# Moving the first routing table, the step-2 transposes and the loop's gathers and transposes in a three-part transformer kernel

## The chip, the cores and the metric

The kernel runs on one core of a Trainium2 chip. The metric is device time in microseconds (us), taken over three runs of the kernel; beside it stands one execution that the hardware profiler recorded. TensorE is PE in the rows (PEld is its weight load), VectorE is DVE, ScalarE is ACT, GpSimd is POOL, and SyncE is SP, whose sequencer issues most of the DMAs.

## The reference

Three operations follow one another. The input is `q`, `k`, `v` of 4 batches, 8 heads, 768 positions and 64 dimensions, with 8 memory keys and values per head.

```python
attn = banded_attention(q, k, v, mem_k, mem_v)         # chunks of 32, 16 left, 8 right, plus memory
x = attn.transpose(0, 2, 1, 3).reshape(3072, 512)
h = x @ w_in                                           # 512 x 2048
g = np.where(h >= 1, h, np.where(h <= -1, 0, (h + 1) ** 2 / 4))
x = g @ w_out                                          # 2048 x 512
logits = normed(x) @ normed(expert_emb).T / tau        # 8 experts
e = argmax(logits); gate = softmax(logits)[e]
out = gate * (np.maximum(x @ w1[e], 0) @ w2[e])        # 512 x 1024 x 512 for each token's expert
```

## The kernel before

Tokens are cut into 8 blocks of 384 (`NB`, three tiles of 128 each). For a block, PE runs attention, then the first layer in 16 chunks of 128 features (`l1_mm`, 12 matmuls of 384 columns per chunk, line 444), then the second layer (`l2_mm`, lines 470 to 472). Each chunk of the first layer leaves PSUM by five instructions: ACT at line 450, DVE at 456 and 460, ACT at 463, DVE at 466. Its PSUM tile comes from a ring of three (`mm`) or of two (`PT`) and is free again when DVE has done line 456. After a block the tokens are routed: `g_logit`, `g_first`, `g_pos` find each token's expert and its rank in that expert.

The experts then run in steps of 256 tokens of one expert. Steps 0 and 1 take only tokens of the first 18 tiles (`TA = 18`, blocks 0 to 5), so that they can begin before block 7 is routed. Their tokens are looked up by the first routing table, the tasks `fac` to `fat`: a count on PE, the keys and places on DVE (`fa_key`, `fa_look`, `fa_place`, the last writes tile `fasv`), 18 small matmuls on PE that gather the token numbers (`fai`, function `fa_ids`, line 940), and the table itself on DVE (`fat`, function `fa_table`, 12 instructions, lines 955 to 1009). The second table (`fbc` to `fbt`) does the same for steps 2 and up.

A step `s` needs four things. `gather(s)` (POOL, line 1130) fetches its token rows from DRAM into `xg`. `transposes(s)` or the task `inputs(s)` (SP, line 1142) turns `xg` into `xhl` by two DMA transposes. `load_w` (SP, lines 1111 and 1113) brings eight pieces of an expert's weights of 512 KB each into `stg`; from step 2 on a piece is loaded only where the expert differs from the one before. `split_w` (ACT, line 1117) and `split_lo` (DVE, line 1122) cut each piece into two f16 halves, into the buffers `wi` for even steps and `wo` for odd ones. Then PE runs four chunks of the first product (`m2_l1`, lines 1156, 1157, 1159), each drained by ACT at 1165 and DVE at 1170, and eight parts of the second (`m2_l2`, lines 1185 to 1187), scaled by ACT at 1194 and stored by POOL at 1197.

Each engine runs its instructions in the order in which they were recorded, and SP's queue does so too: a transpose that waits for its gather holds all loads recorded behind it. Up to and with step 2 and the weight splits of step 3 the order comes from a planner (`Plan`): tasks with needs and costs (`COST`) are listed, and a schedule by those costs sets the order on every engine. From step 3 on the order is written out by hand: `at(n, f, ...)` calls `f` when PE's n-th part is recorded, and a step has 12 such parts, starting at `p = first2 + 12 * s`. In step `s` the loop records the split of piece `c` of the next step at part `1 + c`, the reload of its buffer one part later, the gather of the next step and its transposes.

Of the kernel before, what the change touches and what calls it, by code (L numbers as in the profile page):

```python
# [20 lines left out]
B, H, S, D = 4, 8, 768, 64  # L21
# [10 lines left out]
TB = BT // 128  # L32
# [16 lines left out]
    td=1.25, avc=1.3, avp=0.68, av=0.52, xh=0.38, xl=0.47, ca=(0.58, 0.43), cv=0.34, cb=0.6, cs=0.6, cc=0.53, cd=0.6,  # L49
    l1=0.98, r4=0.47, mu=0.47, mn=0.47, hi=0.43, lo=0.47, l2=1.95, l2t=1.3, x2=0.49, sq=0.62, x2l=0.6, xt=1.25, dot=0.65,  # L50
    pad=0.4, emb=0.5, esq=0.6, ert=0.9, ein=1.9, etr=0.4, ehi=0.2, elo=0.2, grt=0.9, gno=1.6, glo=1.2, gfi=1.5, gst=0.8,
    grk=0.1, gpo=1.7, ga=2.6, w=2.3, wh=0.95, wl=1.13, xd=1.25, m1=2.62, mh=0.49, ml=0.6, m2=1.3, mo=0.57, ms=1.0, fbc=0.193,
    fbk=2.2, fbm=1.87, fbl=3.4, fbp=2.1, fbi=0.7, fbt=3.4, fac=0.175, fak=2.6, fal=1.4, fap=0.42, fai=0.5, fat=1.436)
LAT = (0.25, 1.7, 0.1)
WIN = 0.019
# [98 lines left out]
def moe_chain(ctx, tc, qd, kd, vd, win, wout, emb, tau, w1, w2, tmask, kmask, qp, kp, cf32, cf16, out):  # L154
# [506 lines left out]
    def mixture():  # L661
# [4 lines left out]
        def add(k, n, f, where, needs=(), cost=None, ring=None, frees=()):  # L666
            done[k, n] = pl.add((k, n), f, where, COST[cost or k], [x if isinstance(x, dict) else done.get(x) for x in needs], ring, frees)
# [85 lines left out]
        def inputs(s, needs):  # L753

            old = {0: [], 1: [("l1", NB - 1, NFC - 1, 1)], 2: [("m1", 0, 3), ("mo", (0, 1))]}[s]
            for i in range(2):
                add("xd", (s, i), lambda w, i=i: (i == 0 and t_new(s), t_dma(s, i)), "S", [("ga", s), ("xd", (s, i - 1)), *old, *needs])
# [36 lines left out]
        for j in range(NB):  # L794
            i = start[j] + 2 * NFC
            if j == 0:
                for c in range(NFC):
                    conv(c)
            if j == NB - 1:
                n = (("fat", 0),)  # L800
            else:
                n = ()
            for fc in range(NFC if j != 1 else 0):
                first(j, fc, n)
                if j == NB - 1 and fc == 0:
                    for h in range(2):
                        add("ga", h, lambda w, h=h: gather(h), "G", [prev, ("ga", h - 1)])
                    for c in range(8):
                        add("w", c, lambda w, c=c: load_w(0, c), "S", [prev, ("w", c - 1)])
                if j == NB - 1 and fc % 2 == 1:  # L810
                    weights(0, fc // 2, [prev])
                    if fc == NFC - 1:
                        inputs(0, [prev])
            if j + 1 < NB and j != 1:
                for u in range(UB * (j + 1), UB * (j + 2)):
                    attention(u)
            if j == 0:
                for c in range(NFC, 2 * NFC):
                    conv(c)
                for fc in range(NFC):  # L820
                    k = dict(ring="mm", frees=[("x2l", t) for t in range(TB)]) if fc == 0 else {}
                    pe_slot(("l2", 0, fc), i + fc, [("cd", NFC + fc), ("lo", fc), ("hi", fc)], "l2", **k)

                    if fc >= AHEAD:
                        first(1, fc - AHEAD)
                for fc in range(NFC - AHEAD, NFC):
                    first(1, fc)
                for u in range(2 * UB, 3 * UB):
                    attention(u)
                cds = [("cd", c) for c in range(2 * NFC)]  # L830
                add("pad", 0, lambda w: pads(), "G", cds)
                add("emb", 0, lambda w: emb_load(), "S", [("cf", 0)])
                add("esq", 0, lambda w: emb_sq(), "A", [("emb", 0)])
                add("ert", 0, lambda w: emb_root(), "G", [("esq", 0)])
                add("ein", 0, lambda w: emb_inv(), "D", [("ert", 0)])
                add("etr", 0, lambda w: emb_tr(), "P", [("ein", 0)], ring="mm", frees=[("elo", 0)])
                add("ehi", 0, lambda w: emb_hi(), "A", [("etr", 0)])
                add("elo", 0, lambda w: emb_lo(), "D", [("ehi", 0)])
            for t in range(TB):
                n = TB * j + t  # L840
                if j > 0:
                    for fc in range(0, NFC, 2):
                        m = NFC * j + fc
                        k = dict(ring="mm", frees=[("x2l", n)]) if fc == 0 else {}
                        pe_slot(("l2", j, t, fc), i, [("lo", m), ("lo", m + 1)], "l2t", **k)
                        i += 1
                last = ("l2", j, t, NFC - 2) if j else ("l2", 0, NFC - 1)
                add("x2", n, lambda w, n=n: l2_ev(n, p2[n % TB]), "A", [last, ("gst", j - 2), ("x2", n - 1), ("pad", 0)])
                add("sq", n, lambda w, n=n: g_sq(n, p2[n % TB]), "A", [("x2", n), ("sq", n - 1), ("glo", j - 2)])
                add("x2l", n, lambda w, n=n: l2_lo(n, p2[n % TB]), "D", [("x2", n), ("sq", n)])  # L850
                add("xt", n, lambda w, n=n: g_xt(n), "S", [("x2l", n), ("dot", j - 1), ("xt", n - 1)])
            add("grt", j, lambda w, j=j: g_root(j), "G", [("sq", n)])
            add("gno", j, lambda w, j=j: g_norm(j), "D", [("grt", j), ("ein", 0)])
            add("dot", j, lambda w, j=j: g_dot(j), "P", [("xt", n), ("elo", 0), ("gno", j)], ring="mm", frees=[("glo", j)])
            add("glo", j, lambda w, j=j: g_logit(j), "D", [("gno", j), ("dot", j), ("gpo", j - 2), ("gst", j - 2)])
            add("gfi", j, lambda w, j=j: g_first(j), "D", [("glo", j), ("gfi", j - 1)])
            add("gst", j, lambda w, j=j: g_store(j), "D", [("gfi", j)])
            add("grk", j, lambda w, j=j: g_rank(j), "P", [("gfi", j), ("mk", 0)], ring="mm", frees=[("gpo", j)])
            add("gpo", j, lambda w, j=j: g_pos(j), "D", [("grk", j), ("gpo", j - 1)])
            if (j + 1) * TB == TA:  # L860
                add("fac", 0, lambda w: fa_count(), "P", [("gfi", j)], ring="S", frees=[("fak", 0)])
                add("fak", 0, lambda w: fa_key(), "D", [("fac", 0)])
                add("fal", 0, lambda w: fa_look(), "D", [("fak", 0), ("gpo", j)])
                add("fap", 0, lambda w: fa_place(), "D", [("fal", 0)])
                add("fai", 0, lambda w: fa_ids(), "P", [("fap", 0)], ring="S", frees=[("fat", 0)])
                add("fat", 0, lambda w: fa_table(), "D", [("fai", 0)])
        for c in range(8):
            weights(1, c, [("l2", NB - 1, TB - 1, 2 * c)])
        inputs(1, [])
# [10 lines left out]
        second(1)  # L880
        for c in range(8):
            weights(2, c, [("fbt", 0), ("m1", 0, 3) if c < NK else ("m2", 0, 1, c - NK)])
        inputs(2, [])
        second(2)
        for c in range(8):
            weights(3, c, [("m1", 1, 3) if c < NK else ("m2", 1, 1, c - NK)])
# [77 lines left out]
    def fa_count():  # L964
        fa["c"] = T(ps, [128, NE], F32, "S", 2)
        pe.matmul(fa["c"], ones, rs[:, TA, :], start=True, stop=True)

    def fa_key():
        f = small(NE, "faf")
        rounded(f, fa["c"], -127.5, 1.0 / ST)  # L970
        cum = running(cf[:, C_TR:C_TR + 64].rearrange("p (e f) -> p e f", e=NE), f, "fac")
        b = small(NE, "fab")
        dve.tensor_tensor(b, cum, f, ALU.subtract)
        na = small(NE, "fana")
        dve.tensor_scalar(out=na, in0=b, scalar1=-1.0, scalar2=float(NSTA), op0=ALU.mult, op1=ALU.add)
        dve.tensor_tensor(na, na, f, ALU.min)
        dve.tensor_scalar(out=na, in0=na, scalar1=0.0, scalar2=2.0, op0=ALU.max, op1=ALU.mult)
        dve.tensor_scalar(out=f, in0=f, scalar1=2.0, scalar2=None, op0=ALU.mult)
        dve.tensor_scalar(out=b, in0=b, scalar1=2.0, scalar2=None, op0=ALU.mult)
        fa.update(na2=na, cum=cum, b=b, f=f)  # L980

    def fa_look():
        kb, ft = looked(TA, (fa["b"], "fakb"), (fa["f"], "faft"))
        dve.tensor_tensor(kb, kb, q7a[:, 0:TA], ALU.add)
        dve.tensor_tensor(ft, q7a[:, 0:TA], ft, ALU.is_ge)
        dve.scalar_tensor_tensor(out=kb, in0=ft, scalar=100.0, in1=kb, op0=ALU.mult, op1=ALU.add)
        fa.update(kb=kb)

    def fa_place():
        fa["sv"] = placed(fa["kb"], TA, 2 * NSTA, "fa")  # L990

    def fa_ids():
        fa["ip"] = ids_mm(fa["sv"], TA, 2 * NSTA)
# [221 lines left out]

    for s in range(NSTA, NST0 - 1):
        p = first2 + SL * s
        for c in range(8 if s > NSTA else 0):
            split_at(p + 1 + c, s + 1, c)
        at(p + 1, gather, s + 1)  # L1220
        at(p + 5, transposes, s + 1)

    p2 = {}

# [134 lines left out]
```

## Time and profile before

| | |
|---|---|
| time, median of three runs (lowest to highest) | 931.65 us (930.45 to 932.08) |
| the profiled execution: its own time | 933.45 us |
| its span, from the first to the last instruction | 931.7 us |
| PE busy | 867.6 us (93%) |
| DVE busy | 693.2 us (74%) |
| ACT busy | 557.2 us (60%) |
| POOL busy | 73.7 us (8%) |
| mean granted TensorE clock | 0.993 |

Busy shares are means over the whole span. PE's is high from the first eighth of the span to its end, while the others change from stage to stage, so the places that matter are those at which PE stood idle or ran at its lower clock.

### The profile page before, as it was taken

The page shows a single profiled execution, that of the slowest core. Times are in us where ns is not written, and L with a number is a line of the kernel's source. Part 1 is how long each engine was busy: PE and PEld are TensorE (multiplying, and loading weights), DVE is VectorE, ACT ScalarE, POOL GpSimd, SP SyncE. Part 2 cuts the span into 40 slices and gives each one's busy share as a digit, 9 for nine tenths or more (in the row PEclk, how much of TensorE's full clock was granted, in tenths as well). Part 3 has the DMA queues.
Part 4 walks back from the last instruction along what each step waited for, and adds up shares of the span by engine and source line. Part 5 has one row for each costly group of instructions (what it writes and reads, how often), then busy time and mean ns, then how long its engine had stood idle before and what let it go on. Part 6 is the DMA issues. An engine that isn't in the chain of part 4 may idle for free. (4 is left out here: it accounts for less than half of the span.)

```text
span 931.7 us, 17019 instructions
## 1 busy us (share of the span) xinstructions
PE 867.6 (93%) x6072; PEld 522.0 (56%) x6072; DVE 693.2 (74%) x1600; ACT 557.2 (60%) x1398; POOL 73.7 (8%) x70
## 2 busy tenths in 40 slices
PE   2899999999998999999999989999998999999985
PEld 2766555545544644555554544555665667666653
DVE  6999999999999998988872780795745655566550
ACT  4768757979887858749653341465145555555541
POOL 0000100000000000000000100200122222222210
PEclk9999999999999999999999999999999999999998
DMA  9986513767277437424112001583232232223540
GB/s 255 237 178 202 183 62 99 170 190 175 64 159 208 107 99 183 99 89 81 32 44 49 12 35 30 187 238 91 69 82 68 63 87 70 69 69 81 156 140 25
DMA packets 118700, 105.64 MB, mean 113 GB/s; under 512 B 92286, under 2 KB 92548, under 8 KB 118608
## 3 DMA queue, kind: packets, MB, share of 16 engines
q1 hardware_dynamic: 114608, 91.80, 38.3%
q0 software_dynamic: 4000, 12.69, 4.3%
q8 instruction: 49, 0.80, 0.4%
q14 instruction: 43, 0.35, 0.1%
HBM read 112.09 MB, written 12.94 MB: 134 GB/s over the span
## 5 line engine op out<-in xcount | busy, mean ns | idle before, releaser
L444 PEld LDWEIGHTS <-wi 128*128 128x128 f16 x1536 | 148.2, 99 | 98.9 <-issue 5.7
L444 PE MATMUL mm<-xhl,wi 128*128 128x384 f16 x912 | 160.7, 328 | 1.2 <-ACT xhl L383 0.6
L470 PE MATMUL mm<-wo,g 128*128 128x512 f16 x384 | 146.1, 381 | 0.0
L471 PE MATMUL mm<-wo,g 128*128 128x512 f16 x384 | 145.6, 379 | 0.0
L472 PE MATMUL mm<-wo,g 128*128 128x512 f16 x384 | 145.5, 379 | 0.0
L444 PE MATMUL PT<-xhl,wi 128*128 128x384 f16 x624 | 111.3, 331 | 0.0
L1170 DVE SCALAR_TENSOR_TENSOR g<-PT,g 128x512 f16<-128x512 f32 (+1 forms) x52 | 34.8, 670 | 94.2 <-ACT g L1165 94.2
L463 ACT ACTIVATE g<-r 128x384 f16<-128x384 f32 x128 | 66.9, 523 | 60.6 <-DVE r L460 60.3
L1165 ACT ACTIVATE g<-PT 128x512 f16<-128x512 f32 (+1 forms) x52 | 30.2, 580 | 72.8 <-PE PT L1159 72.8
L1122 DVE SCALAR_TENSOR_TENSOR wi<-stg,wi 128x1024 f16<-128x1024 f32 x56 | 66.0, 1219 | 7.9 <-ACT wi L1117 7.9
L466 DVE TENSOR_TENSOR g<-r,g 128x384 f16<-128x384 f32 x128 | 70.3, 549 | 1.0 <-ACT g L463 0.6
L460 DVE SCALAR_TENSOR_TENSOR r<-r,t 128x384 f32<-128x384 f32 x128 | 70.5, 551 | 0.3
L345 ACT ACTIVATE ab<-e,rc 96x128 f16<-96x128 f32 x184 | 58.7, 398 | 16.7 <-issue 11.2
L309 ACT ACTIVATE e<-S,mx 96x128 f32<-96x128 f32 x184 | 64.2, 363 | 5.6 <-DVE mx L293 5.4
L472 PEld LDWEIGHTS <-g 128*128 128x128 f16 x384 | 37.6, 98 | 45.5 <-issue 0.3
L1122 DVE SCALAR_TENSOR_TENSOR wo<-stg,wo 128x1024 f16<-128x1024 f32 x48 | 56.4, 1220 | 8.4 <-ACT wo L1117 8.0
L470 PEld LDWEIGHTS <-g 128*128 128x128 f16 x384 | 37.5, 98 | 38.6 <-issue 0.2
L471 PEld LDWEIGHTS <-g 128*128 128x128 f16 x384 | 37.6, 98 | 36.0
L479 DVE SCALAR_TENSOR_TENSOR x2a<-mm,x2a 128x512 f16<-128x512 f32 x24 | 16.4, 684 | 55.1 <-ACT junk L487 55.0
L1117 ACT ACTIVATE wi<-stg 128x1024 f16<-128x1024 f32 x56 | 56.9, 1047 | 0.6 <-DMA stg<-w 0.6
L1194 ACT ACTIVATE o<-mm,xg 128x512 f32<-128x512 f32 x25 | 17.2, 687 | 66.2 <-issue 41.9
L450 ACT ACTIVATE r<-mm,two 128x384 f32<-128x384 f32 x76 | 43.8, 577 | 19.5 <-PE mm L444 16.1
(262 smaller groups left out, 1791.5 us busy)
## 6 DMA issues: line engine op xcount, KB each, us to landing
stg<-w SPq DMA_DIRECT2D x104, 512.0 KB
kraw<-kd SPq DMA_DIRECT2D x23, 512.0 KB
qraw<-qd SPq DMA_DIRECT2D x23, 384.0 KB
vraw<-vd SPq DMA_DIRECT2D x30, 256.0 KB
x2d<-x2a SPq DMA_DIRECT2D x8, 780.0 KB
x2a<-win SPq DMA_DIRECT2D x8, 512.0 KB
x2a<-wout SPq DMA_DIRECT2D x7, 512.0 KB
kraw<-kp SPq DMA_DIRECT2D x7, 256.0 KB
```

The source lines that it names most:

```text
L309: act.activation(e[:QU, i, :], w["s"][:QU, i, :], AF.Exp, bias=nb[:QU, i:i + 1], scale=0.125 if plain(a // 2) else 1.0, accum_out=sm[:QU, ...
L345: act.activation(w["ab"][:QU, 0, i, :], w["e"][:QU, i, :], AF.Copy, scale=w["rc"][:QU, i:i + 1])
L444: pe.matmul(l1p[fc], w[fc][:, k, :], x[:, k, :], start=(part == 0 and n == 0), stop=(part == 1 and n == 5))
L450: act.activation(g32[fc], l1p[fc], AF.Relu, bias=two[:, 0:1], scale=2.0 ** -13)
L460: dve.scalar_tensor_tensor(out=r4, in0=r4, scalar=4.0, in1=t4s.pop(fc), op0=ALU.min, op1=ALU.mult)
L463: act.activation(gh[fc], g32[fc], AF.Copy)
L466: dve.tensor_tensor(gl[fc], g32.pop(fc), gh[fc], ALU.subtract)
L470: pe.matmul(p, gh[fc][:, ts], woh[fc], start=(fc == 0), stop=False)
L471: pe.matmul(p, gh[fc][:, ts], wol[fc], start=False, stop=False)
L472: pe.matmul(p, gl[fc][:, ts], woh[fc], start=False, stop=(fc == NFC - 1))
L1117: act.activation(hi, stg[c], AF.Copy, scale=64.0 if c < NK else 512.0)
L1122: dve.scalar_tensor_tensor(out=lo, in0=stg[c], scalar=sc, in1=hi, op0=ALU.mult, op1=ALU.subtract)
```

## The change

Four edits. The tasks of the first routing table are listed behind block 6's first layer and no longer at the end of block 5, and `fai` has a new need: the second half of chunk 13 of that layer (`("l1", j, NFC - 3, 1)`). The planner's cost of a gather (`ga`) goes from 2.6 to 5.6. Step 2's transposes have a new need: the fourth weight load of that step (task `w` 19). In the loop, the next step's gather is recorded at part 0 and not 1, its transposes at part 3 and not 5.

```diff
-    grk=0.1, gpo=1.7, ga=2.6, ...
+    grk=0.1, gpo=1.7, ga=5.6, ...
@@ after the first layer of block j
+            if j * TB == TA:
+                add("fac", 0, lambda w: fa_count(), "P", [("gfi", j - 1)], ring="S", frees=[("fak", 0)])
+                add("fak", 0, lambda w: fa_key(), "D", [("fac", 0)])
+                add("fal", 0, lambda w: fa_look(), "D", [("fak", 0), ("gpo", j - 1)])
+                add("fap", 0, lambda w: fa_place(), "D", [("fal", 0)])
+                add("fai", 0, lambda w: fa_ids(), "P", [("fap", 0), ("l1", j, NFC - 3, 1)], ring="S", frees=[("fat", 0)])
+                add("fat", 0, lambda w: fa_table(), "D", [("fai", 0)])
@@ at the end of block j
-            if (j + 1) * TB == TA:
-                add("fac", 0, ...) to add("fat", 0, ...): the same six, with fai's needs [("fap", 0)]
@@ step 2
-        inputs(2, [])
+        inputs(2, [("w", 19)])
@@ the loop over steps s
+        at(p, gather, s + 1)
         for c in range(8 if s > NSTA else 0):
             split_at(p + 1 + c, s + 1, c)
-        at(p + 1, gather, s + 1)
-        at(p + 5, transposes, s + 1)
+        at(p + 3, transposes, s + 1)
```

**PE in block 6's first layer.** `PT` and `wi04` are the PSUM tile and the weights of a chunk, `S` and `fasv` those of the table's 18 small matmuls (one pair of 18 shown). Before:

```order
L444 LDWEIGHTS wi14_90
L444 MATMUL PT_7014<-xhl_5538,wi14_90 128x384
L940 LDWEIGHTS rhot_74
L940 MATMUL S_7037<-fasv_7031,rhot_74 128x4
...
L444 LDWEIGHTS wi04_82
L444 MATMUL PT_7064<-xhl_5538,wi04_82 128x384
```

Now:

```order
L444 LDWEIGHTS wi07_85
L444 MATMUL PT_7145<-xhl_5538,wi07_85 128x384
L940 LDWEIGHTS rhot_74
L940 MATMUL S_7157<-fasv_7031,rhot_74 128x4
...
L444 LDWEIGHTS wi17_93
L444 MATMUL PT_7145<-xhl_5538,wi17_93 128x384
```

They stood behind chunk 8 and now stand inside chunk 14, nearly six chunks later. The count on PE and the DVE instructions up to `fasv` keep their places; the 12 of `fa_table` move from behind chunk 8's line 460 to behind chunk 13's, between the evacuations of chunks 13 and 14.

**ACT in steps 2 and 3.** L1117 splits a piece (`wi_81` to `wi_85` are pieces 3 to 7 of step 2, `wo_94` those of step 3, from `stg_7402` on), L1165 drains a chunk of step 2's first product, L1194 is a scaling of step 2's second product:

```order
 L1117 ACTIVATE wi_81<-stg_7405 128x1024
 L1117 ACTIVATE wi_82<-stg_7406 128x1024
-L1165 ACTIVATE g<-PT 128x2x256
-L1117 ACTIVATE wi_83<-stg_7407 128x1024
+L1117 ACTIVATE wi_83<-stg_7407 128x1024
+L1117 ACTIVATE wi_84<-stg_7408 128x1024
 L1165 ACTIVATE g<-PT 128x2x256 x2
-L1117 ACTIVATE wi_84<-stg_7408 128x1024
-L1165 ACTIVATE g<-PT 128x2x256
-L1117 ACTIVATE wi_85<-stg_7409 128x1024
+L1117 ACTIVATE wi_85<-stg_7409 128x1024
+L1165 ACTIVATE g<-PT 128x2x256
```

Pieces 5 and 6 of step 2 now go ahead of the first drain. Behind these rows piece 0 of step 3 stands ahead of the last drain of step 2 and piece 1 behind it; piece 2 moves ahead of the second L1194, so that five splits of step 3 (pieces 3 to 7) stand behind it and not six. DVE's splits move in the same way.

**SP from step 4 on.** `xhl` is the next step's input, `stg` the reloaded pieces of the step after it. Before:

```order
L1113 DMA stg2_7404<-w1 128x1024
L1113 ISA
L1113 DMA stg3_7405<-w1 128x1024
L1142 DMA_TRANSPOSE xhl_9030<-xg0_7410 128x8x128
L1142 DMA_TRANSPOSE xhl_9030<-xg1_7411 128x8x128
```

Now:

```order
L1113 DMA stg1_7403<-w1 128x1024
L1142 DMA_TRANSPOSE xhl_9009<-xg0_7410 128x8x128
L1142 DMA_TRANSPOSE xhl_9009<-xg1_7411 128x8x128
L1113 ISA
L1113 DMA stg2_7404<-w1 128x1024
```

The transposes stand behind two reloads and not four. On POOL the order of gathers and stores is the same as before. Step 3's two transposes stood ahead of all eight loads of step 3 and now stand behind its first; step 2's stood behind its first and second load and now stand behind its fifth and sixth.

## Rows read from the trace of the kernel before

**Rows 1.** The page: busy time (share) and instructions by engine.

```profile
PE 867.6 (93%) x6072; PEld 522.0 (56%) x6072; DVE 693.2 (74%) x1600; ACT 557.2 (60%) x1398; POOL 73.7 (8%) x70
```

**Rows 2.** Waits of PE: engine, tile, line, releaser: total us, times, longest.

```profile
PE S L940 <- DVE fasv L934: 4.1, 1, 4.1
...
PE PT L1156 <- DMA xhl<-xg: 3.2, 1, 3.2
PE PT L1156 <- ACT wo L1117: 1.9, 2, 1.3
```

**Rows 3.** Timeline, PE, block 6's first layer: start, us, instruction, count, [idle before <-releaser].

```profile
532.62 2.11 PE L444 MATMUL PT<-xhl,wi 128*128 128x384 f16 x12
...
538.86 0.61 PE L940 MATMUL S<-fasv,rhot 128*128 128x4 f16 x18 [4.13 <-DVE fasv L934]
539.33 3.77 PE L444 MATMUL PT<-xhl,wi 128*128 128x384 f16 x12
...
552.70 2.11 PE L444 MATMUL mm<-xhl,wi 128*128 128x384 f16 x12
```

**Rows 4.** Stretches: us; PE, PEld, DVE, ACT, POOL busy; granted clock; DMA share, GB/s.

```profile
539.60:543.00 3.40, 3.40 (x13) 1.58 (x11) 3.26 (x13) 0.52 (x1) 0.00 (x0) 0.50 0.62 234
144.50:147.00 2.50, 0.41 (x5) 0.31 (x5) 2.44 (x4) 2.16 (x11) 0.00 (x0) 1.00 0.00 0
147.10:150.40 3.30, 3.30 (x17) 2.09 (x16) 3.29 (x11) 1.33 (x3) 0.00 (x0) 0.50 0.78 246
...
714.00:726.00 12.00, 8.45 (x67) 6.13 (x66) 8.78 (x9) 9.33 (x11) 4.48 (x3) 1.00 0.22 68
```

**Rows 5.** Timeline, DVE, block 6's first layer.

```profile
540.82 0.55 DVE L456 SCALAR_TENSOR_TENSOR t<-PT,r 128x384 f32<-128x384 f32 x1
...
542.22 0.17 DVE L955 TENSOR_TENSOR faet<-fac,cf 128x16 f32<-128x16 f32 x1
...
544.21 0.55 DVE L456 SCALAR_TENSOR_TENSOR t<-PT,r 128x384 f32<-128x384 f32 x1
...
545.80 0.56 DVE L456 SCALAR_TENSOR_TENSOR t<-mm,r 128x384 f32<-128x384 f32 x1
```

**Rows 6.** Timelines, ACT, DVE and PE, steps 2 and 3.

```profile
697.29 0.60 ACT L1165 ACTIVATE g<-PT 128x512 f16<-128x512 f32 x1 [2.00 <-PE PT L1159]
716.15 5.78 ACT L1117 ACTIVATE wo<-stg 128x1024 f16<-128x1024 f32 x6
697.92 0.69 DVE L1170 SCALAR_TENSOR_TENSOR g<-PT,g 128x512 f16<-128x512 f32 x1 [1.18 <-ACT g L1165]
717.23 6.90 DVE L1122 SCALAR_TENSOR_TENSOR wo<-stg,wo 128x1024 f16<-128x1024 f32 x6 [3.95 <-ACT wo L1117]
699.71 0.27 PE L1156 MATMUL PT<-xhl,wi 128*128 128x256 f16 x1
724.78 0.27 PE L1156 MATMUL PT<-xhl,wo 128*128 128x256 f16 x1 [0.93 <-DVE g L1170]
```

**Rows 7.** PE, SP and POOL before step 11; DMA issues with median us to landing.

```profile
889.58 0.27 PE L1156 MATMUL PT<-xhl,wo 128*128 128x256 f16 x1 [3.16 <-DMA xhl<-xg]
876.05 0.35 SPq L1113 DMA_DIRECT2D stg<-w  x1
880.17 4.67 SPq L1142 DMA_TRANSPOSE xhl<-xg  x2
885.17 2.72 SPq L1113 DMA_DIRECT2D stg<-w  x4
869.30 1.02 POOL L1130 DMA_INDIRECT xg<-x2d,fbid  x1 [0.31 <-issue]
xg<-x2d,fbid POOLq DMA_INDIRECT x21, 3.5
```

**Rows 8.** Stretches in the columns of rows 4: step 10's transposes alone; around step 11's start.

```profile
860.00:863.30 3.30, 3.30 (x17) 1.51 (x16) 3.30 (x3) 1.63 (x2) 1.71 (x1) 1.00 0.83 159
...
886.00:892.00 6.00, 2.84 (x25) 2.20 (x24) 0.00 (x0) 0.69 (x1) 1.61 (x2) 1.00 1.05 322
```

More of the change, by code (lines that the diff above doesn't have):

```diff
@@ L51 @@
     pad=0.4, emb=0.5, esq=0.6, ert=0.9, ein=1.9, etr=0.4, ehi=0.2, elo=0.2, grt=0.9, gno=1.6, glo=1.2, gfi=1.5, gst=0.8,
-    grk=0.1, gpo=1.7, ga=2.6, w=2.3, wh=0.95, wl=1.13, xd=1.25, m1=2.62, mh=0.49, ml=0.6, m2=1.3, mo=0.57, ms=1.0, fbc=0.193,
+    grk=0.1, gpo=1.7, ga=5.6, w=2.3, wh=0.95, wl=1.13, xd=1.25, m1=2.62, mh=0.49, ml=0.6, m2=1.3, mo=0.57, ms=1.0, fbc=0.193,
     fbk=2.2, fbm=1.87, fbl=3.4, fbp=2.1, fbi=0.7, fbt=3.4, fac=0.175, fak=2.6, fal=1.4, fap=0.42, fai=0.5, fat=1.436)
@@ L859, in mixture @@
             add("gpo", j, lambda w, j=j: g_pos(j), "D", [("grk", j), ("gpo", j - 1)])
-            if (j + 1) * TB == TA:
[L861 to L866, printed above, removed]
         for c in range(8):
```

## The prediction, made before the changed kernel had run

> **What bounds the kernel now.** I read the page first: PE is busy in 93% of the span [rows 1], so a change pays only where PE stands idle or runs at its lower clock. The list of PE's waits then says where that is [rows 2]. Its longest waits stand at the start of the program, which the change does not touch. Behind them come 4.13 us for `fasv` in block 6's first layer, one wait of 3.16 us for a DMA transpose, and waits for weight splits. I looked at each in the timelines.
>
> In block 6 PE ends chunk 8 at 534.73 (532.62 + 2.11) and stands until 538.86, because the 18 small matmuls come next in its order and DVE has not finished their operand [rows 3]. The 12 matmuls of the chunk behind it take 3.77 us, where 12 take 2.11 later in the same layer [rows 3]. [...]
>
> Before step 3 PE waits for splits of step 3's weights: six run back to back on ACT behind the last scaling of step 2, and six on DVE from 717.23 to 724.13. The drains of the first product come behind them, and PE waits for a drain until 724.78 [rows 6]. Before step 11 PE waits until 889.58 for the step's input [rows 7]: SP issued the two transposes from 880.17 on, behind four real weight loads, and took 4.67 us for it; the DMA engines show a share of 1.05 around that time [rows 7, 8].
>
> **The change, part by part.**
>
> *First table.* Nothing is added or removed: 18 matmuls on PE and 12 instructions on DVE move. PE no longer stops behind chunk 8; it reaches the 18 matmuls inside chunk 14, some 5.5 chunks later. A chunk takes 1.95 us (12 matmuls in 2.11, of which the last 0.16 overlaps the next), so PE comes there at 534.6 + 5.5 x 1.95 = 545.3, and `fasv` was ready at 538.8: no wait. The gain is the wait, 4.13, plus the slow clock, 3.77 - 2.11 = 1.66, plus the 0.16 of overlap that a stop costs: **5.9 us**. The 18 matmuls' half microsecond is paid in either place.
>
> What could be late next is DVE. It takes chunk 8's tile at 540.82 [rows 5], 6.1 us behind PE, and from there a chunk every 1.59 us (545.80 - 544.21) against PE's 1.95. PE would stop for a PSUM tile: chunk 13 takes the `PT` tile of chunk 8, free at 541.37, and starts at 534.6 + 4 x 1.95 = 542.4; chunk 14 takes chunk 9's, free 1.59 later at 543.0, and starts at 544.3. So 1.0 and 1.3 us are to spare. The table's 12 instructions (542.22 to 544.21, 2.0 us) [rows 5] now stand between chunks 13 and 14, where no further first-layer tile waits for them. The second layer's first tile reads chunks 14 and 15 in its last of eight parts; the seven ahead hold 42 matmuls of 512 columns, by an estimate from 0.163 us per 384 columns 9.1 us. DVE's lag there is 6.1 - 7 x 0.36 + 2.0 = 5.6 us. I keep 5.9; the low end is 3.0, if the spare microsecond is gone and PE stops for a tile two or three times, and the high end 6.1. The gathers and loads that read the table come only with block 7, a whole second layer later, and everything that hangs on PE's progress moves with it.
>
> *The gather's cost and step 2's transposes.* Both work only through the planner. Step 2's own transposes I cost at nothing: PE's only wait for a transpose is the one before step 11 [rows 2], and while their gather is on its way SP may as well issue loads. The gain is on ACT and DVE. ACT was idle 2.00 us ahead of step 2's first drain at 697.29 [rows 6]; pieces 5 and 6 (0.96 us apiece back to back: six take 5.78) now fill that. So step 3's splits start earlier, and five and not six stand behind step 2's last scaling. On DVE six splits take 6.90, 1.15 apiece, so the drain that PE waits for until 724.78 [rows 6] comes one split earlier. The cost: DVE's drain of step 2's first chunk, which ran from 697.92 to 698.61, now stands behind two more splits, which begin where DVE fell idle: 697.92 - 1.18 + 2 x 1.15 + 0.69 = 699.73. PE needs its tile at 699.71 [rows 6], so the cover is just used up. Ends: 0.5 (a wait of half a microsecond there) and 1.3; I take **1.1 us**. The wait of 1.9 in all for `wo` [rows 2] does not go: pieces 3 and up still stand behind the scaling.
>
> *Gather and transposes in the loop.* On POOL nothing changes place, so the gather comes no earlier. On SP the transposes pass two reloads. In steps 4 to 10 PE did not wait for them, so this gives nothing there; the reloads are not needed (a piece is reloaded where the expert changes). Before step 11 the reloads are real. The transposes' turn comes behind the second of them, issued at 876.05 [rows 7], so at 876.5 and not 880.17. Their gather was issued until 870.32 and lands 3.5 us later in the median [rows 7], by 873: it does not hold them. A transpose pair alone keeps the DMA engines busy for 3.3 us at 159 GB/s [rows 8], the 512 KB load ahead of it takes 1.6 to 2.2 at the 322 and 234 GB/s of full queues [rows 4, 8]. So the data is there at about 876.4 + 2.2 + 3.3 = 881.9, or, from the other side, as long after the issue as before (889.58 - 884.84 = 4.74, with four loads in the queue): 876.5 + 4.67 + 4.74 = 885.9. PE is ready at 889.58 - 3.16 = 886.42. Both ends lie before that, so the whole wait goes: **3.3 us** with the overlap. The six loads behind the transposes now start later by at most one pair, but the last four were held by the pair before (885.17 [rows 7]), and their splits run a step later. The low end is 0, if the transposes are still late; the high end 3.4.
>
> *Sum.* 5.9 + 1.1 + 3.3 = 10.3 us. Against the profiled execution, 933.45 us (span 931.7), that is 923.1; against the median of the runs, 931.65, it is **921.3 us**, 1.1% less.
>
> **The clock.** In the trace a wait does not always bring the clock down. From 144.50 to 147.00 PE was idle for 2.1 of 2.5 us, and the clock was 0.50 from 147.10 to 150.40; from 714 to 726 it was idle for 3.5 of 12 us in several pieces and the clock stayed 1.00, as it did behind the 3.16 us before step 11 [rows 4, 8]. So a wait that stays, such as those for `wo` in steps 2 and 3 [rows 2], may bring it down when all comes 6 us earlier, at 1.66 us a time. [...] I keep it as a rival.
>
> **The rivals.**
> 1. *The transposes are still late before step 11*: the queue is as full as before, since two loads in front still move 1 MB. For it: the DMA share of 1.05 [rows 8]. Against it: both ends above. 921.3 + 3.3 = **924.6 us**.
> 2. *PE's wait comes back on DVE*: spare times of 1.0 and 1.3 us are thin, and DVE is busy for nearly all of that stretch (3.26 of 3.40 us [rows 4]). At the low end of 3.0 it is **924.2 us**.
> 3. *The clock falls at a remaining wait*: **923.0 us**.
> 4. *Slower*: the transposes now stand at the head of SP's queue with six real loads of step 12 behind them. If the gather were late they would hold those loads, and PE would wait at step 12. The gather lands 3.5 us ahead of the transposes' turn, and the last loads, issued until 887.89 [rows 7], are split only during step 11. To lose more than the 10.3 and 1.9 us besides, the gather must land over 25 us late; nothing in [rows 7] comes near. **934 us**.
> 5. *The plan's edits do not do what they say* and neither wait goes: about 931 us. The order on PE and SP shows that both stretches did move.
>
> **How the numbers follow.** Forecast 0.72, rival 1 0.09, rival 2 0.08, rival 3 0.06, rival 4 0.02, rival 5 0.03. The range's low end is 919.8: the high ends of the three parts (10.8) and the spread of the runs below their median (up to 1.2, of which I take half). Its high end is 924.6, which takes in rivals 1 to 3; what is left out, with the tails of the forecast, is under 2 in 10. About 0.2%, 1.9 us, is what a measurement of this kernel can tell from no change. Faster by more than that are the forecast and rivals 1 to 3: 0.95. The same: rival 5, 0.03. Slower: rival 4, 0.02.
>
> **What would show it.** In the profile after: no wait for `fasv` and a granted clock of 1.00 through block 6; the 18 small matmuls about 5.5 chunks behind chunk 8; six chunks of a first layer without a wait for DVE's line 456; step 3's last DVE splits as a run of five; a drain-bound wait 1.1 us earlier relative to step 3's start; transposes of step 11 ahead of the third real load, and no wait at step 11. The forecast is wrong if PE waits on a first-layer tile in block 6, if line 1156 still waits for `xhl`, or if the clock falls in a stretch where it was full.

## The result, and the profile after

The changed kernel takes 921.66 us (median of five runs, 920.69 to 922.24); the kernel before, run beside it, 932.04 us (930.45 to 932.08). The ratio is 0.9896, with a 95% interval from 0.9883 to 0.991. The forecast was 921.3 us, with a range of 919.8 to 924.6. The profiled execution took 920.69 us, with a span of 918.9.

The page, in the columns of [rows 1]: the same work, PE idle for less of a shorter span.

```profile
PE 862.9 (94%) x6072; PEld 520.1 (57%) x6072; DVE 691.9 (75%) x1600; ACT 556.5 (61%) x1398; POOL 74.6 (8%) x70
```

The waits of PE, in the columns of [rows 2]. Neither `fasv` nor `xhl` is in that list now, and the wait for `wo` fell from 1.9 to 1.1 us. Those that lead among the steps:

```profile
PE PT L1156 <- DVE g L1170: 1.6, 2, 0.9
...
PE PT L1156 <- ACT wi L1117: 1.1, 1, 1.1
PE PT L1156 <- ACT wo L1117: 1.1, 1, 1.1
```

PE's timeline in block 6, against [rows 3]. The first chunk on `PT` and its neighbour are chunks 8 and 9, the second group of `PT` starts with chunk 13, and the 18 small matmuls stand inside chunk 14 with no idle time ahead of them:

```profile
530.41 4.06 PE L444 MATMUL PT<-xhl,wi 128*128 128x384 f16 x24
534.31 6.01 PE L444 MATMUL mm<-xhl,wi 128*128 128x384 f16 x36
540.16 3.09 PE L444 MATMUL PT<-xhl,wi 128*128 128x384 f16 x18
543.08 0.59 PE L940 MATMUL S<-fasv,rhot 128*128 128x4 f16 x18
543.54 1.14 PE L444 MATMUL PT<-xhl,wi 128*128 128x384 f16 x6
```

The stretches, in the columns of [rows 4]: PE is busy for all of block 6's first layer, at the full clock.

```profile
530.40:546.50 16.10, 16.10 (x117) 9.88 (x115) 15.27 (x47) 7.26 (x16) 0.00 (x0) 1.00 0.13 51
```

DVE there, against [rows 5]: the tiles of chunks 8, 9 and 12, and the table's first instruction, now behind chunk 13.

```profile
538.47 0.55 DVE L456 SCALAR_TENSOR_TENSOR t<-PT,r 128x384 f32<-128x384 f32 x1
540.06 0.56 DVE L456 SCALAR_TENSOR_TENSOR t<-PT,r 128x384 f32<-128x384 f32 x1
...
544.80 0.56 DVE L456 SCALAR_TENSOR_TENSOR t<-mm,r 128x384 f32<-128x384 f32 x1
...
547.84 0.17 DVE L955 TENSOR_TENSOR faet<-fac,cf 128x16 f32<-128x16 f32 x1
```

ACT and DVE in steps 2 and 3, against [rows 6]: runs of five splits where there were six, and DVE's drain of step 2's first chunk at 690.73, behind two splits more.

```profile
707.95 4.83 ACT L1117 ACTIVATE wo<-stg 128x1024 f16<-128x1024 f32 x5
```

```profile
690.73 0.68 DVE L1170 SCALAR_TENSOR_TENSOR g<-PT,g 128x512 f16<-128x512 f32 x1
...
709.02 5.77 DVE L1122 SCALAR_TENSOR_TENSOR wo<-stg,wo 128x1024 f16<-128x1024 f32 x5 [3.95 <-ACT wo L1117]
```

SP before step 11, against [rows 7]: two loads, the transposes, six loads. And PE at step 11's start (876.92), which follows the last matmul of step 10 without a stop:

```profile
864.10 2.98 SPq L1113 DMA_DIRECT2D stg<-w  x2
867.19 3.85 SPq L1142 DMA_TRANSPOSE xhl<-xg  x2
871.41 4.29 SPq L1113 DMA_DIRECT2D stg<-w  x6
```

```profile
876.71 0.38 PE L1187 MATMUL mm<-wi,g 128*128 128x512 f16 x1
876.92 0.27 PE L1156 MATMUL PT<-xhl,wo 128*128 128x256 f16 x1
```

The DMA engines around these transposes are hardly less full than in [rows 8], with a share of 0.98 against 1.05. What changed is when the transposes run: they were issued 11.1 us after step 10's start and not 14.75, and their last packets ended 16.5 us after it and not 22.0.

```profile
867.20:873.00 5.80, 5.80 (x28) 2.65 (x27) 5.61 (x6) 4.95 (x7) 0.04 (x1) 1.00 0.98 205
```

The two profiled spans differ by 12.8 us, 2.4 us more than the medians. Up to the table's count on PE (line 966, one matmul in block 6, which the change does not move) the executions already differ by 2.2 us: 0.84 at the start of the program, 0.70 for a clock that fell at 147 us in one and not in the other, and 0.67 around block 5's routing (the last section has both). Up to the count every engine has its instructions in the same order in both kernels, so none of that is counted as the change's, and from here on stretches are compared and not spans.

### The profile page after: what moved, and what is told of

Read it like the earlier page. It is cut to its first block, busy times and chain, and to the rows that moved or that the text cites. A ratio compares the mean times of both kernels' runs of the same rounds, so it can differ in the third digit from the quotient of the medians.

```text
span 918.9 us, 17019 instructions
## 1 busy us (share of the span) xinstructions
PE 862.9 (94%) x6072; PEld 520.1 (57%) x6072; DVE 691.9 (75%) x1600; ACT 556.5 (61%) x1398; POOL 74.6 (8%) x70
## 5 line engine op out<-in xcount | busy, mean ns | idle before, releaser
L444 PE MATMUL PT<-xhl,wi 128*128 128x384 f16 x624 | 108.6, 326 | 0.0
L1165 ACT ACTIVATE g<-PT 128x512 f16<-128x512 f32 (+1 forms) x52 | 30.2, 580 | 67.4 <-PE PT L1159 67.3
L1194 ACT ACTIVATE o<-mm,xg 128x512 f32<-128x512 f32 x25 | 17.2, 687 | 67.1 <-issue 42.9
L1117 ACT ACTIVATE wi<-stg 128x1024 f16<-128x1024 f32 x56 | 56.7, 1047 | 0.0
L350 DVE SCALAR_TENSOR_TENSOR ab<-e,rc,ab 96x128 f16<-96x128 f32 x184 | 52.6, 341 | 2.7 <-ACT ab L345 2.7
```

The source lines that it names most:

```text
L350: dve.scalar_tensor_tensor(out=w["ab"][:QU, 1, i, :], in0=w["e"][:QU, i, :], scalar=w["rc"][:QU, i:i + 1], in1=w["ab"][:QU, 0, i, :], op0= ...
L444: pe.matmul(l1p[fc], w[fc][:, k, :], x[:, k, :], start=(part == 0 and n == 0), stop=(part == 1 and n == 5))
L1117: act.activation(hi, stg[c], AF.Copy, scale=64.0 if c < NK else 512.0)
```

## The experiments

The table gives the stretches that the change touches, from PE's timeline in one profiled execution each, in us: from the count (line 966) to step 1's first matmul, which holds block 6's first layer, and the lengths of steps 2, 3 and 10 (first matmul to first matmul of the next). A step in which PE never stops takes 20.84 us.

| kernel | count to step 1 | step 2 | step 3 | step 10 | ratio to before (95%) |
|---|---|---|---|---|---|
| before | 142.33 | 22.85 | 25.07 | 24.16 | |
| after | 136.34 | 22.85 | 23.93 | 20.84 | 0.9896 (0.9883 to 0.991) |
| e5_after, the same again | 136.35 | 22.85 | 23.93 | 20.84 | 0.9896 (0.9878 to 0.9915) |
| e1_table, edit 1 alone | 136.34 | 22.85 | 25.65 | 23.07 | 0.9937 (0.9924 to 0.9951) |
| e2_loop, edit 4 alone | 142.30 | 22.85 | 25.06 | 20.84 | 0.999 (0.998 to 1.0) |
| e3_w19, edit 3 alone | 142.32 | 22.84 | 23.93 | 22.44 | 1.0004 (0.9991 to 1.0017) |
| e4_ga, edit 2 alone | 142.94 | 22.85 | 25.06 | 22.06 | 1.0002 (0.999 to 1.0013) |
| e9_rest, edits 2, 3 and 4 | 142.19 | 22.84 | 23.93 | 20.84 | 0.9964 (0.995 to 0.9978) |
| e8_half | 141.36 | 22.85 | 23.93 | 20.84 | 0.9949 (0.9933 to 0.9966) |
| e12_nine | 137.58 | 22.85 | 23.93 | 20.84 | |
| e7_dve | 138.49 | 22.84 | 23.93 | 20.84 | |
| e10_four, e11_one | 136.34 | 22.85 | 23.93 | 20.84 | |
| e6_splits | 136.35 | 20.84 | 20.84 | 20.84 | 0.9845 (0.9829 to 0.9861) |

### One edit at a time

**e1_table**: the kernel before with the table's six tasks behind block 6's first layer, and nothing else.

> The kernel before with the first edit alone: the first table's tasks behind block 6's first layer. The forecast's first term says 5.9 us less than the kernel before (wait of 4.13, slow clock 1.66, overlap 0.16): no wait for fasv, and a granted clock of 1.00 through block 6. If the wait comes back on DVE (rival 2) the gain is 3.0 us and PE waits for line 456 two or three times. If the wait alone were what matters and the slow clock came from elsewhere, the gain is 4.3 us and the clock is still 0.50 for some 3.4 us in block 6.

The stretch is 142.33 - 136.34 = 5.99 us shorter, and the ratio of 0.9937 is 5.9 us of 930. No wait for `fasv`, none for line 456, the full clock: the first term stands by itself. The same profile shows rival 3 elsewhere, in step 3: the clock fell at a wait for `wo` that it had survived in [rows 4].

```profile
530.00:546.00 16.00, 16.00 (x116) 9.82 (x114) 15.24 (x50) 6.91 (x15) 0.00 (x0) 1.00 0.13 50
714.00:717.40 3.40, 3.40 (x19) 2.40 (x17) 3.40 (x4) 3.11 (x4) 1.48 (x1) 0.50 0.51 154
```

It cost 25.65 - 25.07 = 0.58 us, not the 1.66 of the prediction: the wait of 0.93 for a drain, which came next, was gone (PE's waits for line 1170 are 1.6 us in two in the kernel before, 0.7 in one here). I read it as DVE catching up while PE ran slowly.

**e2_loop**: the kernel before with `at(p, gather, ...)` and `at(p + 3, transposes, ...)`.

> The kernel before with the fourth edit alone: in the loop the gather at part 0 and the transposes at part 3. The forecast's third term says 3.3 us less than the kernel before, all of it before step 11: no wait of line 1156 for xhl, and steps 4 to 10 as they were. If the transposes are still late behind two real loads (rival 1) the difference is 0 and the wait stands. If loads held behind the transposes matter, PE waits for wi or wo in step 12.

The wait is gone (step 10 takes 20.84 us). Yet the median is only 0.1% below that of before, between 0 and 1.9 us. One reason is in the executions that kept the old order. Their first matmul of step 11, for e3_w19:

```profile
887.05 0.27 PE L1156 MATMUL PT<-xhl,wo 128*128 128x256 f16 x1 [1.44 <-DMA xhl<-xg]
```

and for e4_ga, with SP's queue ahead of it, which is that of [rows 7]:

```profile
887.21 0.27 PE L1156 MATMUL PT<-xhl,wo 128*128 128x256 f16 x1 [1.06 <-DMA xhl<-xg]
```

```profile
873.16 6.62 SPq L1113 DMA_DIRECT2D stg<-w  x4
879.90 4.26 SPq L1142 DMA_TRANSPOSE xhl<-xg  x2
```

Four executions with one order show waits of 3.16, 2.06, 1.44 and 1.06 us. Loads and transposes were issued at the same times from step 10's start to within half a microsecond; what differs is when the data had landed. The transposes' last packets ended 22.0 us after step 10's start where PE waited 3.16 us, and 20.6 us after it where PE waited 1.06 (in the other two they ended at 21.4, with waits of 2.06 and 1.44, so the last packet alone does not fix the wait). In the execution with the longest wait, packets of the store of step 10's output ran among them from 20.2 to 22.5 us, in the one with the shortest for 0.8 us. That the store delays them is a reading of two traces, not shown by an experiment. The old order cost 1.2 to 3.3 us of step 10, 2.1 in the mean of four. That is still above the 1.9 us to which the interval of the medians reaches; what the clock adds to it stands under e9_rest.

On POOL the order with the gather at part 0 is that of before row for row, and a gather is recorded on POOL alone, so the gather's move does nothing.

**e3_w19**: the kernel before with `inputs(2, [("w", 19)])`.

> The kernel before with the third edit alone: step 2's transposes need the step's fourth load; the gather's cost stays at 2.6. The order on ACT and DVE then already shows what the two planner edits gave together: pieces 5 and 6 ahead of the first drain of step 2, five splits and not six behind its last scaling. If this need is the whole cause, it is 1.1 us less than the kernel before, at the wait for a drain in step 3. If the gather's cost matters too, it is less than that; if an earlier set of transposes was what PE lived on, PE waits for xhl in step 2 and the time is the same or longer.

Step 3 is 1.14 us shorter, to the same 23.93 as in the changed kernel, so this edit is the whole cause of the second term. The waits of PE in step 3:

```profile
717.58 0.28 PE L1156 MATMUL PT<-xhl,wo 128*128 128x256 f16 x1 [1.12 <-ACT wo L1117]
718.84 0.28 PE L1159 MATMUL PT<-xhl,wo 128*128 128x256 f16 x1 [0.54 <-DVE wo L1122]
723.97 0.27 PE L1156 MATMUL PT<-xhl,wo 128*128 128x256 f16 x1 [0.92 <-DVE g L1170]
```

The median does not show it: 1.0004, and its interval reaches only to 0.8 us faster. The trace says 1.1.

**e4_ga**: the kernel before with `ga=5.6`.

> The kernel before with the second edit alone: the planner's cost of a gather at 5.6. On PE the order is that of before, on ACT and DVE no row changes place in steps 2 and 3; only on SP the step 2 transposes pass one load each. If the third edit is the whole cause of the second term, this gives 0 (within 0.5 us of the kernel before). If the gather's cost carries the term, it is 1.1 us less.

Nothing in step 3 (25.06 us), nothing in the median. The gather's cost does no work here.

**e9_rest**: the changed kernel with the table put back, to settle whether the small terms are real.

> The changed kernel with the first edit undone: the kernel before with the planner's cost, the need of step 2's transposes and the loop's two moves. It asks whether the small terms are there, which single kernels did not show in their medians (0.999 for the loop, 1.0004 for the need). By the step lengths of the traces (25.06 to 23.93 us for step 2, 24.16, 23.07, 22.44 or 22.06 to 20.84 for step 10) the two are worth 1.13 + 2.1 = 3.2 us, a ratio of 0.9965 to the kernel before, and the kernel is 5.9 us slower than the changed one. By the medians of the single kernels they are worth 0.5 us, a ratio of 0.9995, and the table with the rest is worth over 8 us.

(Where this text gives 25.06 to 23.93 us for step 2, it is step 3.) The ratio is 0.9964, that is 3.3 us (2.0 to 4.7), and it is what the traces said, not what the medians of the single kernels said. With the table's 0.9937 the product is 0.9901, against 0.9896 measured for the whole. Why the three single medians together show only some 0.4 us is not settled. Each of these kernels has executions spread over 3 to 5 us, and the last section names three causes of spread that an execution has or has not.

The clock is one of them, and every execution has its mean granted clock on record. In the traces it is 0.997 without a stretch at the low clock, 0.994 or 0.995 with one of 3.41 us and 0.992 or 0.993 with two. Ten of e3_w19's twelve executions had 0.990 or 0.991, against 14 of 29 of before. Among e2_loop's, the seven at 0.991 took 929.18 to 930.63 us and the five above it 927.44 to 928.90. At 0.991 alone the means are 931.10 us for before (six executions), 929.96 for e2_loop (seven), 930.22 for e3_w19 (eight) and 931.23 for e4_ga (three): there the loop and the need show, and the gather's cost does not. At the other values the differences to before scatter from 1.75 us faster to 1.3 slower, so this makes the small terms likelier and does not measure them.

**e5_after**: the whole change once more, beside before on the chip of the next experiments.

> The whole change, beside the same runs of the kernel before as the next kernels. The single edits gave 5.9 us for the table, 0.7 for the loop and nothing for the planner's need and cost. If the terms simply add, the whole change gives the table's 5.9, the planner's 1.1 (30.38 to 29.24 us from step 2's to step 3's second phase in the traces) and, before step 11, the wait that is there: 3.16, 2.06, 1.44 and 1.06 us in the four traces with the old order, mean 1.9. That is 8.9 us. If the forecast's full 3.3 us is the rule, it is 10.3; if only what the single kernels showed in the medians is real, 6.6.

921.67 us against 930.69; the ratio is 9.7 us (7.9 to 11.4). The sum of the terms, 5.99 + 1.14 + 2.1 = 9.2 us, lies within that, and so does 10.3: the runs agree with terms that add, and cannot tell the two sums apart.

### What a wait costs in block 6

**e8_half** and **e12_nine**: the changed kernel with `fai`'s need on chunk 8 or 9 in place of 13. The table's instructions on DVE move with it.

```diff
-                add("fai", 0, lambda w: fa_ids(), "P", [("fap", 0), ("l1", j, NFC - 3, 1)], ...)
+                add("fai", 0, lambda w: fa_ids(), "P", [("fap", 0), ("l1", j, 8, 1)], ...)
```

> The changed kernel with the table's 18 matmuls half a chunk behind chunk 8 (need on chunk 8 and not 13): PE then waits 4.13 - 0.98 = 3.15 us for fasv. Against the changed kernel it is 3.3 us more if the granted clock stays at 1.00, as it did behind the wait of 3.16 us before step 11, and 5 us more if the clock falls to 0.50 for some 3.4 us, as it did behind 4.13 us in block 6.

> The changed kernel with the table's 18 matmuls behind the first half of chunk 10 (need on chunk 9): PE then waits 4.13 - 0.98 - 1.95 = 1.2 us for fasv. In the traces so far the clock fell at this place at every wait of 3.16 us or more (six executions) and PE's waits of 1.06 to 3.16 us before step 11 never brought it down. If what decides is that PE stands idle for 3 us at this place, the clock stays at 1.00 and the cost over the changed kernel is 1.4 us; if shorter waits here do it as well, it falls for some 3.4 us and the cost is 3 us.

PE in e8_half, and the stretch behind the wait:

```profile
539.37 0.60 PE L940 MATMUL S<-fasv,rhot 128*128 128x4 f16 x18 [3.16 <-DVE fasv L934]
```

```profile
540.40:543.70 3.30, 3.30 (x12) 1.55 (x11) 3.20 (x13) 1.63 (x3) 0.00 (x0) 0.50 0.64 242
```

The same two for e12_nine:

```profile
538.25 0.61 PE L940 MATMUL S<-fasv,rhot 128*128 128x4 f16 x18 [1.07 <-DVE fasv L934]
```

```profile
540.40:543.70 3.30, 3.30 (x22) 2.00 (x21) 3.13 (x8) 1.69 (x4) 0.00 (x0) 1.00 0.61 231
```

At 3.16 us of idle time the clock fell and the stretch is 5.02 us longer than in the changed kernel; at 1.07 us it stayed and the stretch is 1.24 us longer. Subtracting the waits leaves 1.86 and 0.17 us: the overlap that a stop costs, 0.17, and 1.69 for the slow clock. That is the prediction's split of the first term, 4.13 + 1.66 + 0.16, taken apart by experiment. The 3.16 us in block 6 brought the clock down and the 3.16 us before step 11 [rows 7, 8] did not, so the length of the wait alone does not decide.

### How far DVE and the transposes are from being late

**e7_dve**: the changed kernel, with 12 more copies of one DVE instruction ahead of chunk 7's tile.

```diff
-        dve.tensor_tensor(sv, ..., ALU.is_equal)
+        for _ in range(13 if tag == "fa" else 1): dve.tensor_tensor(sv, ..., ALU.is_equal)
```

> The changed kernel with the first of the two instructions that write fasv (DVE, line 933) issued 13 times and not once, 12 more of some 0.15 to 0.23 us: D = 1.8 to 2.8 us more of DVE work ahead of chunk 7's tile. It measures rival 2's margin. In the changed kernel's trace chunk 12's matmuls start 1.3 us after DVE has freed their tile and chunk 13's 1.1 us. If DVE is the next bound, PE waits in all D - 1.1 us for line 456 at chunks 12 and 13. If there is far more to spare, PE does not wait. If there is none, it waits D.

DVE and PE in its block 6:

```profile
537.11 3.43 DVE L933 TENSOR_TENSOR fasv<-cf,fakb 128x72 f16<-128x72 f32 x13
```

```profile
542.82 0.55 DVE L456 SCALAR_TENSOR_TENSOR t<-PT,r 128x384 f32<-128x384 f32 x1
```

```profile
541.33 2.11 PE L444 MATMUL mm<-xhl,wi 128*128 128x384 f16 x12 [1.83 <-DVE t L456]
543.42 3.09 PE L444 MATMUL PT<-xhl,wi 128*128 128x384 f16 x18
```

3.43 us in place of 0.23 are 3.2 us more, and PE waited 1.83 of them at chunk 12, so 1.37 us were to spare there. Chunk 13 came late as well: DVE freed its tile at 543.37 (542.82 + 0.55), and it started at 543.42, 2.09 us behind chunk 12 and not 1.95. In all the stretch became 138.49 - 136.34 = 2.15 us longer, as D - 1.1 had it. Rival 2's mechanism exists; the change stays clear of it by 1.1 us, at chunk 13.

**e10_four** and **e11_one**: the changed kernel with the loop's transposes at part 4 or 1.

```diff
-        at(p + 3, transposes, s + 1)
+        at(p + 4, transposes, s + 1)
```

> The changed kernel with the loop's transposes at part 4 and not 3, behind three reloads and not two. The packets of step 11's transposes ended 16.5 us behind step 10's mark in the changed kernel's trace, and 20.6 and 22.0 us behind it in two traces with four reloads ahead; PE could go on some 1.5 us behind that and needs the data at 20.84. If each real load ahead costs about 2.3 us, the packets end at 18.3 to 19.3 and PE does not wait, with 0 to 1 us to spare. If the wait is set by something other than the loads ahead, it is back at 1 to 3 us.

> The changed kernel with the loop's transposes at part 1, ahead of all eight reloads. It puts rival 4 to its hardest test: the transposes wait for a gather issued only a part or two earlier, and all loads stand behind them. If the hold is short (the gather's packets ended 7.4 us behind step 10's mark, the first real load was issued at 8.0) step lengths from step 4 on stay at 20.84 us. If loads held behind the transposes matter, step 11 or step 12 is longer than 20.84 and PE waits for wi or wo there.

Neither has a wait at step 11 or 12. Behind three loads the transposes' packets ended 19.85 us after step 10's start, later than I had put them and with next to nothing to spare before 20.84. At part 1 they stand ahead of all eight loads on SP:

```profile
862.85 2.70 SPq L1142 DMA_TRANSPOSE xhl<-xg  x2
867.66 8.27 SPq L1113 DMA_DIRECT2D stg<-w  x8
```

The first load's packets then started 12.0 us after step 10's start and not 9.0, and step lengths stayed at 20.84. Rival 4's hold happened and was harmless: the loads are needed much later.

### A kernel faster than both

**e6_splits**: the changed kernel, with a lower planner's cost for loads from step 2 on.

```diff
-    ... w=2.3, wh=0.95, ...
+    ... w=2.3, w2=1.0, wh=0.95, ...
@@ weights(s, c, needs)
-                add("w", 8 * s + c, lambda w: load_w(s, c), "S", [...])
+                add("w", 8 * s + c, lambda w: load_w(s, c), "S", [...], cost="w2" if s > 1 else None)
```

> The changed kernel with one thing more: the planner's cost of a weight load from step 2 on is 1.0 and not 2.3 (w2=1.0). PE's order stays; on ACT pieces 2 to 4 of step 2 and pieces 2 to 6 of step 3 are split ahead of the last scaling of the step before, on DVE as well. If the splits were late only because the plan put them behind a scaling (their loads were issued in 0.07 to 0.08 us each, against 0.35 for a load before step 11), PE's waits of 1.12 and 0.54 at the start of step 2, 1.12 and 0.54 at step 3 and 0.92 at its drain go, and it is 4.2 us less than the changed kernel. If the splits now hold scalings or drains back, PE waits for a PSUM tile of the second product instead and it is the same or longer. If the data in the staging buffers comes later than assumed, the waits stay.

916.67 us against 921.67 for the changed kernel beside it: 5.0 us less, and 14.4 us less than before (12.9 to 15.9). Steps 2 and 3 take the 20.84 us of a step without a stop. ACT between them, to be read against the run of six in [rows 6]: the splits lie in pairs ahead of the scalings (line 1194), where ACT had been idle.

```profile
696.45 1.99 ACT L1117 ACTIVATE wo<-stg 128x1024 f16<-128x1024 f32 x2
701.18 0.69 ACT L1194 ACTIVATE o<-mm,xg 128x512 f32<-128x512 f32 x1 [2.74 <-issue]
701.77 1.99 ACT L1117 ACTIVATE wo<-stg 128x1024 f16<-128x1024 f32 x2
706.36 0.69 ACT L1194 ACTIVATE o<-mm,xg 128x512 f32<-128x512 f32 x1 [2.60 <-issue]
706.95 1.99 ACT L1117 ACTIVATE wo<-stg 128x1024 f16<-128x1024 f32 x2
```

I had expected 4.2 us, the sum of the listed waits. The steps became 2.01 + 3.09 = 5.1 us shorter: each of the five stops also cost some 0.17 us of overlap. With these data the loads of steps 2 and 3 are skipped (issued in 0.07 us each, against 0.35 for a real one in [rows 7], and without a packet of theirs in the trace), so the plan waited for loads that were not made. With data that switch the expert there it could come out otherwise; that was not tried.

## Why the prediction was right, and where it was only nearly so

**First table: 5.9 forecast, 5.99 measured.** The slow clock in the term is the 0.50 granted from 539.60 to 543.00 [rows 4]. All three parts of the term were there: e8_half and e12_nine give the wait at its own length, 1.69 for the clock and 0.17 for the stop. The place came out as worked out too: the 18 matmuls were put at 545.3 and came at 543.08, and the execution was ahead by 2.21 us at the count. DVE held: spare times of 1.0 and 1.3 us were forecast for chunks 13 and 14; chunk 13 started 1.14 us after DVE had freed its tile (540.16 against 538.47 + 0.55), and e7_dve found 1.37 us at chunk 12 and 1.1 at chunk 13.

**Planner's edits: 1.1 forecast, 1.14 measured**, by the mechanism named: DVE's run of splits shorter by one. The third edit does it alone; the prediction had costed the two together and could not tell them apart. The cover called "just used up" was so: the drain forecast for 699.73 ended at 691.41, and with the 8.2 us by which step 2 came earlier that is 699.61, 0.1 us ahead of need. The wait for `wo` was said not to go; it did not, but shrank from 1.9 to 1.1 us.

**Gather and transposes: 3.3 forecast, 3.32 between the two profiled executions, but 1.2 to 3.3 over four with the old order.** This is the term that was mis-sized. The bounds for the arrival (16.5 to 20.5 us after step 10's start) held, with the last packets at 16.5, and the whole wait went; what failed is that the length of a DMA wait was read from one execution as if it were the kernel's. That execution was 1.8 us above the median of its runs, and the prediction subtracted all 10.3 us from the median all the same. With 2.1 in place of 3.3 the sum is 9.2 us and the forecast 922.4; measured were 921.66 and 921.67.

**Two sums that do not come out.** The range's low end is 931.65 - 10.8 - 0.6 = 920.25 by its own terms, and not 919.8. The gather's landing, 870.32 + 3.5, is 873.8 and not 873, which is still ahead of the transposes' turn at 876.5. Neither touches the forecast, and the measured time lies inside either range.

**The rivals.** Late transposes (1) and DVE (2) did not come, with margins now measured. The clock (3) fell at a remaining wait in one execution of e1_table and in none of those of the changed kernel's steps 2 and 3 that a trace shows; its price there was 0.58 and not 1.66 us, because a wait stood right behind. One of the five executions behind the result, at 922.24 us, has a mean clock of 0.993, where the two traces of the changed kernel have 0.997 and 0.995; so the clock probably fell once more in it, and no trace shows where. The hold on SP (4) cost nothing even with the transposes ahead of all loads. Of (5), that edits do not do what they say, a part is true: the gather's cost and the gather's move change no time.

## What to carry to other kernels

In block 6 and in the steps a wait of PE on another engine repeated to 0.2 us or better from execution to execution (3.98 to 4.13 us for `fasv` in four traces), and could be costed from one trace; the wait for the DMA transposes behind four loads did not (1.06 to 3.16 us), and wants several traces or a range from its own spread before it goes into a sum against a median. In block 6 a stop cost its wait plus 0.17 us (e12_nine) and, where the rows show that the clock fell, 1.69 more (e8_half). And when a planner sets the order, look for engines that stand idle beside work that is ready: a cost for loads that the data make unnecessary was worth 5 us here, half as much as the whole change.

## What the runs showed of the hardware

**The same wait may or may not bring the clock down.** At 144 to 149 us PE stops for 1.7 us in every execution, in all but one for 0.5 us just ahead of it, in code that no kernel here touches. The granted clock fell there in 11 of 14 profiled executions, for 3.41 us each, and not in the other three. The stretch behind the wait in after, where it stayed:

```profile
147.10:150.40 3.30, 2.85 (x18) 1.42 (x17) 3.30 (x11) 2.83 (x11) 0.00 (x0) 1.00 0.72 266
```

and in e5_after, the same kernel, where it fell (the stretch begins 0.2 us earlier, right behind the fall in that execution):

```profile
146.90:150.20 3.30, 3.30 (x14) 1.79 (x13) 3.30 (x12) 1.70 (x5) 0.00 (x0) 0.50 0.78 271
```

The three that kept the clock are those in which it was first granted in full at 53.24, 53.29 and 53.74 us; in the eleven others that was at 53.82 to 55.77. So in these 14 traces the executions that paid can be told from the others by about 54 us, long before the work that the change moves. The nearest two on either side are only 0.08 us apart, no experiment shows that the one sets the other, and why the same wait has two outcomes is not shown. Where the clock fell, the way from 97 us to the count was 0.73 us longer (430.1 in e5_after against 429.37 in after), not the 1.7 of block 6, in part since a wait of 0.45 us behind it was absorbed.

**In block 6 the low clock lasted longer once.** At waits of 3.16 to 4.13 us it fell in all six executions, for 3.41 us in five and 6.83 in one (e4_ga), which made the stretch from the count to step 1 0.6 us longer than in the others with the table in its old place.

**A small DVE instruction beside POOL's memsets took one of two lengths.** A third spread of 0.7 us lies in blocks 5 and 6 ahead of the count: two waits of 0.20 and 0.16 us, seen with before, e1_table, e2_loop, e3_w19 and e8_half and not with the other nine, whose instructions stand in the same order there. It begins at one DVE instruction of the routing, line 507, which runs while POOL fills four buffers (line 902). In before:

```profile
517.92 1.95 POOL L902 MEMSET xg<- 128x520 f32 x4
518.00 1.88 DVE L507 TENSOR_SCALAR nsa<-nsa 128x3 f32<-128x3 f32 x1 [0.24 <-POOL nsa L502]
```

and in after:

```profile
516.38 1.96 POOL L902 MEMSET xg<- 128x520 f32 x4
516.47 0.94 DVE L507 TENSOR_SCALAR nsa<-nsa 128x3 f32<-128x3 f32 x1 [0.24 <-POOL nsa L502]
```

It took 1.88 or 1.89 us in those five executions and 0.94 in the nine, against 0.13 to 0.17 in the eight other places of before where that line runs, with no memset of POOL beside it. So the waits go with this instruction's length. That the memsets hold it up is a reading of the traces; no experiment moved them, and why one execution gets the longer of the two lengths stays open.
